# More products of a constant tile on TensorE, in the old places and in new ones

## The chip, the cores and the metric

The kernel runs on one core of a Trainium2 chip. The metric is the time of one execution on the device in microseconds. TensorE (PE) multiplies, VectorE (DVE) and ScalarE (ACT) work on what it leaves in PSUM, GpSimd (POOL) is used at the start alone, and SyncE (SP) issues the DMAs. PEld stands for TensorE's weight loads, which overlap its products.

## What is computed

Attention with a position bias, and a feed-forward layer behind it:

```python
rel = pos[:, None] - pos[None, :]                      # S = 576
x = (log1p(|rel|) / log1p(max(pos[:, None], 1)))[..., None]
bias = relu(x @ w1 + b1) @ w2                          # 1 -> 32 -> 8 heads
scores = q @ k.T / sqrt(64) + bias                     # 4 batches, 8 heads
attn = exp(scores - max) / (sum + 1e-9)
x = (attn @ v) as 2304 tokens x 512
h = x @ w_in                                           # 512 -> 2048
out = (h * sigmoid(1.702 h)) @ w_out                   # 2048 -> 512
```

Inputs and output are float32. The kernel computes most products as three float16 products of split numbers (high times high, high times low, low times high).

## The kernel before, in words

The work is cut into tasks, each for one engine, with the tasks that it depends on and the buffers that it takes and gives back. A planner (class `Plan`) runs a model of the engines over them and returns one list, `plan.seq`; the kernel then issues the instructions of that list in order, so that each engine executes its own tasks in the order of the list. The numbers that decide the order are a table of priorities (`TURNS`); the change leaves it alone.

The stages, as the trace shows them:

- The **bias**: relu of the hidden layer on ScalarE and VectorE (L636, L638), products with w2 on TensorE (`products`, L662), eviction to SBUF (L674, L676), a store to a scratch tensor in DRAM and a load back that turns it by position (L683, L732). It is spread over the first 180 us, and begins the program.
- **q and k**: loaded, split and transposed, the first ones on TensorE (L771 for q, L845 and L846 for k), the others by DMA.
- The **weights** w_in and w_out: loaded by SyncE (L1227), put together and split on VectorE (L1234, L1238, L1242, L1260, L750) and ScalarE (L1258), in the first 150 us.
- **Units** u = 0, 1, 2, ...: one block of 128 rows of one pair of heads. Each has scores on TensorE (`scores`, L983), a reduction with the bias on VectorE (L992), exp on ScalarE (L1001), normalisation, a transposition and attention times V. The first eight units transpose on TensorE (`turn_pe`, L1051 and L1054, copied out at L1060 and L1066) and multiply with V in float32 (`av_direct`, L1077); the later ones are transposed by DMA and go in pairs (`av`, L1101). The result is split at L1117, L1119 and L750.
- The **feed-forward layer**: `m1` (L1311), gating on ScalarE and VectorE (L1319, L1325, L1333, L1335, L1340) and `m2` (L1352), in blocks of 256 tokens. It begins at 103 us and goes on to the end.

PSUM has a tile `sp` of four banks, two tiles `hp`, and a tile `op` of two banks.

**Fill products.** Ahead of some tasks of TensorE the kernel issues products of a constant tile `less` (written once by GpSimd) with itself. Nobody reads their result; it goes to the right half of the second `hp` tile, of which the tasks in question use the left half. The table `WARM` (L444) gives their number by the place of the task among TensorE's tasks, counted from 0:

```python
WARM = {2: 22, 3: 18, 7: 3, ...}

def fill(n, fn):
    def both():
        for _ in range(n):
            nc.tensor.matmul(h_tiles[1][:, 256:512], lhsT=less[:, 0],
                rhs=less.rearrange("p z n -> p (z n)"), start=True, stop=True)
        fn()
    return both

pieces = [t for t in plan.seq if t["eng"] == "PE"]
for i, n in WARM.items():
    pieces[i]["fn"] = fill(n, pieces[i]["fn"])
```

They are put in after the planner has run, so the planner doesn't know of them. In the profile they have line 1413. TensorE executes its products in order: a task behind a run of fills starts after it.

Of the kernel before, what the change touches and what calls it, by code (L numbers as in the profile page):

```python
# [177 lines left out]
def kernel(  # L178
# [262 lines left out]

    MAKE_AHEAD = 1
    POOL_EXP = set()
    WARM = {2: 22, 3: 18, 7: 3, 12: 4, 15: 4, 17: 5, 18: 10, 19: 10, 31: 4, 33: 4, 51: 5, 54: 5, 86: 8, 89: 24, 90: 14, 91: 2, 95: 6}  # L444

    WIDE, NARROW = 1152, 592
    PITCH = 704
# [962 lines left out]
# [3 lines that stand above are left out]
                nc.tensor.matmul(  # L1413
                    h_tiles[1][:, 256:512], lhsT=less[:, 0], rhs=less.rearrange("p z n -> p (z n)"), start=True, stop=True
                )
            fn()
        return both

    with tc.manual_schedule():
        plan.order()  # L1420
# [3 lines that stand above are left out]
# [56 lines left out]
```

## Time and profile before

| | |
|---|---|
| timed runs | 634.31, 632.13, 633.86 us; median 633.86 |
| profiled execution | 632.81 us; its span 631.0 us |
| busy in the span | TensorE 590.9, VectorE 534.3, ScalarE 377.4 us |
| mean granted clock of TensorE | 0.995 of full speed |
| fill products | 148 |

The span runs from the first to the last instruction; all times below count from its start. A row of the timeline merges equal instructions that follow each other on an engine. [...]

### The profile page before, as it was taken

To read this page: it belongs to the slowest core of one execution; us is meant where nothing else is said; L and a number is where in the kernel's file an instruction comes from. 1 tells how busy PE (TensorE), PEld (TensorE's weight loads), DVE (VectorE), ACT (ScalarE), POOL (GpSimd) and SP (SyncE) were. 2 spreads that over 40 slices of the span, in tenths; PEclk is the share of its full clock that TensorE was granted. 3 is DMA by queue.
4 is the path that set the end of the run, shared out by engine and by line. 5 is a ranking of instruction groups with operands and counts; after the bars stand their busy time and mean duration, and the time that the engine had idled before them with its cause. 6 is when DMAs were issued, how large, how long until landed. Compare 5 with 4: busy or idle time off the path is not lost.

```text
span 631.0 us, 21930 instructions
## 1 busy us (share of the span) xinstructions
PE 590.9 (94%) x9328; PEld 422.5 (67%) x9328; DVE 534.3 (85%) x1446; ACT 377.4 (60%) x836; POOL 4.9 (1%) x22
## 2 busy tenths in 40 slices
PE   7777789997999999999999899999999999999997
PEld 4545456765666667767677676776777677777874
DVE  6989999999999989989889789899797776984442
ACT  7978988788796855554556366467364534452221
POOL 3000000000000000000000000000000000000000
PEclk9989989999999999999999999999999999999999
DMA  9999996689989999999999969979979380652000
GB/s 230 301 298 314 255 253 163 157 214 210 275 228 200 167 255 225 201 188 197 196 220 223 207 154 185 177 167 192 204 154 193 65 158 35 113 116 39 35 3 35
DMA packets 254491, 113.61 MB, mean 180 GB/s; under 512 B 234036, under 2 KB 234168, under 8 KB 254392
## 3 DMA queue, kind: packets, MB, share of 16 engines
q1 hardware_dynamic: 254104, 111.84, 83.1%
q8 instruction: 73, 1.20, 0.8%
q10 hardware_dynamic: 288, 0.35, 0.2%
q14 instruction: 26, 0.21, 0.1%
HBM read 52.26 MB, written 15.61 MB: 108 GB/s over the span
## 4 chain that ended last, share of the span: by engine, by line
PE 72%; DVE 11%; ACT 8%; DMA 6%; issue 2%; POOL 0%; SPq 0%; ACTq 0%; DVEq 0%; POOLq 0%
PE hp L1311 27%; PE op L1352 25%; PE hp L1101 8%; PE sp L983 7%; ACT wide L636 3%; DVE wide L992 2%; PE sp L662 2%; DMA wide<-in_moe_w_in_dram 2%; ACT wide L1001 2%; PE sp L1352 2%; DVE wide L750 1%; DMA narrow<-in_q_dram 1%; DVE narrow L1242 1%; DVE w L750 1%; DVE narrow L1238 1%
## 5 line engine op out<-in xcount | busy, mean ns | idle before, releaser
L1311 PE MATMUL hp<-xT,w 128*64 128x256 f16 x3456 | 204.9, 273 | 1.9 <-DVE xT L750 1.4
L1311 PEld LDWEIGHTS <-w 128*64 128x64 f16 x3456 | 186.7, 110 | 20.3 <-issue 10.9
L1352 PE MATMUL op<-w,gT 128*64 128x512 f16 x1632 | 194.7, 380 | 0.6 <-issue 0.6
L1001 ACT ACTIVATE wide<-wide,sm 128x576 f32<-128x576 f32 x144 | 110.8, 770 | 66.9 <-DVE sm L992 66.2
L1352 PEld LDWEIGHTS <-gT 128*64 128x64 f16 x1728 | 95.6, 110 | 77.6 <-issue 8.2
L992 DVE CUSTOM_DVE_ANT_0 wide<-sp,wide 128x576 f32<-128x576 f32 x144 | 105.1, 752 | 5.8 <-PE sp L983 2.9
L1319 ACT ACTIVATE th<-hp 128x256 f32<-128x256 f32 x144 | 54.3, 379 | 88.8 <-PE hp L1311 74.6
L750 DVE SCALAR_TENSOR_TENSOR wide<-wide,sm,wide 128x576 f16<-128x576 f32 x128 | 102.7, 813 | 2.6 <-ACT wide L1030 2.4
L1325 DVE SCALAR_TENSOR_TENSOR th<-th,hp 128x256 f32<-128x256 f32 x144 | 59.8, 417 | 32.3 <-ACT th L1319 30.9
L983 PE MATMUL sp<-wide,narrow 64*128 64x512 f16 (+2 forms) x720 | 65.0, 318 | 7.3 <-DVE narrow L750 2.7
L1340 DVE TENSOR_TENSOR gT<-th,gT 128x256 f16<-128x256 f32 x144 | 60.3, 421 | 10.1 <-ACT gT L1333 8.1
L1101 PEld LDWEIGHTS <-v 128*64 128x64 f16 x2160 | 57.8, 111 | 7.4 <-issue 4.7
L1101 PE MATMUL hp<-wide,v 128*64 128x128 f16 (+1 forms) x2160 | 60.2, 214 | 2.0 <-issue 2.0
L1030 ACT ACTIVATE wide<-wide,sm 128x576 f16<-128x576 f32 x72 | 54.1, 769 | 12.6 <-DVE sm L1010 10.4
L983 PEld LDWEIGHTS <-narrow 64*128 64x128 f16 (+1 forms) x960 | 28.3, 97 | 43.1 <-issue 22.6
L636 ACT ACTIVATE wide<-tab,bp 128x384 f32<-128x384 f32 (+16 forms) x94 | 56.3, 654 | 0.0
L1333 ACT CAST gT<-th 128x256 f16<-128x256 f32 x71 | 28.4, 400 | 25.9 <-DVE th L1325 14.7
L1028 DVE TENSOR_SCALAR wide<-wide,sm 128x576 f16<-128x576 f32 x56 | 28.4, 514 | 0.3
L1001 ACT ACTIVATION_READ_ACCUMULATOR wide<-wide,sm 128x1 f32 x144 | 27.2, 189 | 0.0
L662 PE MATMUL sp<-wide,pk 128*32 128x512 f32 (+24 forms) x264 | 20.9, 431 | 4.9 <-DVE sm L992 4.6
L1335 DVE CAST gT<-th 128x256 f16<-128x256 f32 x73 | 20.9, 289 | 5.1 <-PE sp L1352 3.5
L1008 DVE TENSOR_SCALAR sm<-sm 128x1 f32<-128x1 f32 (+1 forms) x128 | 18.9, 151 | 5.8 <-ACT wide L1001 5.3
(87 smaller groups left out, 489.3 us busy)
## 6 DMA issues: line engine op xcount, KB each, us to landing
wide<-scr SPq DMA_DIRECT2D x32, 576.0 KB, 5.4
scr<-narrow SPq DMA_DIRECT2D x30, 295.5 KB, 4.5
wide<-in_moe_w_out_dram SPq DMA_DIRECT2D x16, 512.0 KB, 5.6
wide<-in_moe_w_in_dram SPq DMA_DIRECT2D x16, 512.0 KB, 6.2
narrow<-in_q_dram SPq DMA_DIRECT2D x16, 256.0 KB, 4.3
out_dram<-narrow SPq DMA_DIRECT2D x15, 256.0 KB, 2.9
w<-in_v_dram SPq DMA_DIRECT2D x4, 576.0 KB, 6.9
wide<-scr SPq DMA_DIRECT2D x8, 288.0 KB, 4.6
```

The costliest lines, as they stand in the source:

```text
L636: nc.scalar.activation(out=h, in_=tv, func=ACTF.Relu, bias=bp[:, pb:pb + 1])
L750: nc.vector.scalar_tensor_tensor(out=out, in0=in0, scalar=scale, in1=in1, op0=ALU.mult, op1=ALU.subtract)
L983: nc.tensor.matmul(pair[64 * e:64 * e + m, a, cs], lhsT=qt[r, x, hp + e, q0:q0 + m], rhs=k_of(b, hp + e, y, cs)[r], start=i == 0, stop=i == 2,
L992: nc.vector.tensor_tensor_reduce(out=slot(("a32", u))[:, cs], in0=slot(("sp", u)).rearrange("p (h a) n -> p h (a n)", h=2)[:, a, 0:S], in1 ...
L1001: nc.scalar.activation(out=t, in_=t, func=ACTF.Exp, scale=-1.0, bias=sm[:, a:a + 1], accum_out=sm[:, 2 + a:3 + a])
L1030: nc.scalar.activation(out=o, in_=t, func=ACTF.Identity, scale=r)
L1101: nc.tensor.matmul(o[64 * a:64 * a + 64, po], lhsT=vt[:, x, vc:vc + 64], rhs=t[:, 9 * y + k0, po], start=kb < 0 and i == 0, stop=kb == 3 a ...
L1311: nc.tensor.matmul(p[y0:y0 + FF, :n], lhsT=wi16[:, f // 4, cc, z, w0:w0 + FF], rhs=r, start=i == 0, stop=i == 11, skip_group_check=FF < 128,)
L1319: nc.scalar.activation(out=slot(("th", j, f))[:, :n], in_=slot(("hp", j, f))[:, :n], func=ACTF.Tanh, scale=0.851 / (XS * WIS))
L1325: nc.vector.scalar_tensor_tensor(out=th, in0=th, scalar=1.0, in1=slot(("hp", j, f))[:, :n], op0=ALU.add, op1=ALU.mult)
L1340: nc.vector.tensor_tensor(out=gt[:, 1, :n], in0=th, in1=gt[:, 0, :n], op=ALU.subtract)
L1352: nc.tensor.matmul(o_of(j, i)[y0:y0 + FF], lhsT=gt[:, z, 128 * i + y0:128 * i + y0 + FF], rhs=wo16[:, NF - 1 - f, y, :], start=f == 0 and ...
```

## The change

One line: the numbers of `WARM`.

```diff
-    WARM = {2: 22, 3: 18, 7: 3, 12: 4, 15: 4, 17: 5, 18: 10, 19: 10, 31: 4, 33: 4, 51: 5, 54: 5, 86: 8, 89: 24, 90: 14, 91: 2, 95: 6}
+    WARM = {2: 24, 3: 20, 7: 4, 8: 2, 9: 2, 12: 4, 14: 1, 15: 5, 17: 7, 18: 12, 19: 12, 27: 1, 31: 5, 33: 5, 36: 3, 40: 2, 44: 2, 49: 1, 51: 6, 54: 6, 86: 9, 89: 24, 90: 16, 91: 3, 95: 7}
```

148 products become 183. Fifteen entries of the old table grow by one or two, two stay, and eight are new. What the changed entries stand ahead of, with the start of that task in the trace of before:

| entry | task behind the fills | starts at, us | fills before, now |
|---|---|---|---|
| 2, 3 | bias products of chunk 0 | 10.90, 14.14 | 22 to 24, 18 to 20 |
| 7, 8, 9 | bias products of chunk 0 | 20.47, 22.55, 25.18 | 3 to 4, 0 to 2, 0 to 2 |
| 14 | bias product of chunk 1 | 33.12 | 0 to 1 |
| 15 | scores u = 0 | 37.56 | 4 to 5 |
| 17 | bias product of chunk 1 | 41.95 | 5 to 7 |
| 18 | scores u = 1 | 44.54 | 10 to 12 |
| 19 | bias product of chunk 1 | 48.70 | 10 to 12 |
| 27 | bias product of chunk 1 | 57.63 | 0 to 1 |
| 31 | transposes of k | 63.51 | 4 to 5 |
| 33 | transposes of u = 2 | 68.73 | 4 to 5 |
| 36, 40 | attention times V, u = 2 and 3 | 71.17, 75.90 | 0 to 3, 0 to 2 |
| 44 | transposes of k | 82.17 | 0 to 2 |
| 49 | attention times V, u = 5 | 88.93 | 0 to 1 |
| 51, 54 | transposes of u = 6 and 7 | 92.76, 96.65 | 5 to 6, 5 to 6 |
| 86 | scores u = 14 | 138.77 | 8 to 9 |
| 90 | scores u = 15 | 152.30 | 14 to 16 |
| 91 | attention times V, u = 12 and 13 | 153.47 | 2 to 3 |
| 95 | `m2` of f = 9 | 160.63 | 6 to 7 |

Nothing else moves: the other engines have the same instructions in the same order. Two places, as the programs have them (rows with + are new, rows with - are gone; what an instruction waits for stands in brackets).

TensorE at entry 44, ahead of the transposes of k (`sp<-idn,w`), behind the transposes of u = 4 (`hp<-idn`, `op<-idn`):

```order
 L1051 MATMUL hp_124<-idn,wide_84 128x128 [waits Activation_49]
 L1054 MATMUL op<-idn,wide_84 128x128 x4
+L1413 LDWEIGHTS less
+L1413 MATMUL hp_124<-less 128x256
+L1413 LDWEIGHTS less
+L1413 MATMUL hp_124<-less 128x256
 L845 MATMUL sp<-idn,w_63 128x128 [waits DMAHW4_49,DVE_49,Activation_49]
```

The two fills wait for nothing; the wait stays with the first transpose.

TensorE at entry 36, ahead of attention times V of u = 2 (`hp_123<-w`), behind the scores of u = 4 (`sp<-wide,narrow`):

```order
 L983 MATMUL sp<-wide_91,narrow_107 128x64
-L1077 MATMUL hp_123<-w_63 64x128 [waits Activation_49]
-L1077 MATMUL hp_123<-w_63 64x128
+L1413 LDWEIGHTS less
+L1413 MATMUL hp_124<-less 128x256 [waits Activation_49]
+L1413 LDWEIGHTS less
+L1413 MATMUL hp_124<-less 128x256
+L1413 LDWEIGHTS less
+L1413 MATMUL hp_124<-less 128x256
+L1077 MATMUL hp_123<-w_63 64x128 x2
 L1077 MATMUL hp_123<-w_63 64x128 [waits Activation_49]
```

Here the first fill has taken over the wait of the product behind it: ScalarE copies the left half of the same tile, `hp_124`, to SBUF (L1066). The wait of the third product (for the other copy, L1060) stays. Entries 40 and 49 look alike; at entry 27 the first fill waits for VectorE's copy of that tile.

## Rows read from the trace of the kernel before

**Rows 1.** The page, busy time by engine and granted clock in 40 slices.

```profile
PE 590.9 (94%) x9328; PEld 422.5 (67%) x9328; DVE 534.3 (85%) x1446; ACT 377.4 (60%) x836; POOL 4.9 (1%) x22
...
PEclk9989989999999999999999999999999999999999
```

**Rows 2.** Windows by stage: start to end and length, busy us (instructions) by engine, clock, DMA.

```profile
0.00:100.00 100.00, 75.72 (x892) 49.95 (x894) 90.56 (x213) 85.66 (x165) 4.90 (x22) 0.97 0.98 271
...
165.00:625.00 460.00, 454.42 (x7538) 328.03 (x7536) 379.02 (x1079) 239.68 (x556) 0.00 (x0) 1.00 0.81 159
```

**Rows 3.** Timeline of TensorE: start, us, line, tiles, form, count [idle before, releaser].

```profile
25.18 1.34 PE L662 MATMUL op<-wide,pk 128*32 128x111 f32 x24 [0.54 <-ACT wide L674]
...
37.56 1.34 PE L983 MATMUL sp<-wide,narrow 64*128 64x512 f16 x12 [2.68 <-DVE narrow L750]
...
38.83 2.20 PE L662 MATMUL op<-wide,pk 128*32 128x191 f32 x24
...
41.95 1.21 PE L662 MATMUL op<-wide,pk 128*32 128x175 f32 x24
...
44.54 0.91 PE L983 MATMUL sp<-wide,narrow 64*128 64x512 f16 x12 [0.17 <-DVE sm L992]
```

**Rows 4.** Windows of half a microsecond around the two places of low clock.

```profile
38.00:38.50 0.50, 0.50 (x6) 0.24 (x4) 0.47 (x3) 0.33 (x1) 0.00 (x0) 0.50 0.08 33
...
81.50:82.00 0.50, 0.00 (x0) 0.00 (x0) 0.50 (x3) 0.50 (x3) 0.00 (x0) 1.00 0.77 303
...
82.50:83.00 0.50, 0.50 (x5) 0.50 (x4) 0.50 (x3) 0.50 (x2) 0.00 (x0) 0.50 0.98 203
```

**Rows 5.** Timeline of TensorE: runs of fill products, and the first bias product.

```profile
6.34 4.63 PE L1413 MATMUL hp<-less 128*128 128x256 f16 x22
...
10.90 1.24 PE L662 MATMUL op<-wide,pk 128*32 128x15 f32 x24
...
43.09 1.27 PE L1413 MATMUL hp<-less 128*128 128x256 f16 x10
...
142.70 2.79 PE L1413 MATMUL hp<-less 128*128 128x256 f16 x24
```

**Rows 6.** Timeline of TensorE: attention times V of u = 2, its later part.

```profile
72.08 1.09 PE L1077 MATMUL hp<-w 128*64 128x128 f32 x16 [0.47 <-ACT w L1060]
```

**Rows 7.** The chain of waits in order of time: start, us, what.

```profile
8.36 3.89 ACT wide L636 x6
...
12.26 0.71 ACT narrow L674
...
26.34 7.46 DMA wide<-in_moe_w_in_dram
...
56.66 4.18 DMA wide<-in_moe_w_in_dram
...
159.88 0.81 PE hp L1413 x6
```

**Rows 8.** Timeline of TensorE from 82 to 89 us.

```profile
82.17 1.02 PE L845 MATMUL sp<-idn,w 128*128 128x128 f32 x4 [1.06 <-ACT wide L636]
...
84.61 1.91 PE L1077 MATMUL hp<-w 64*64 64x128 f32 x20
...
87.88 0.91 PE L983 MATMUL sp<-wide,narrow 64*128 64x512 f16 x12 [0.22 <-DVE wide L750]
...
88.93 1.46 PE L1077 MATMUL hp<-w 64*64 64x128 f32 x20
```

**Rows 9.** Timeline of TensorE behind the fills at 153 and 160 us.

```profile
153.47 1.86 PE L1101 MATMUL hp<-wide,v 128*64 128x128 f16 x60
...
160.63 2.84 PE L1352 MATMUL op<-w,gT 128*64 128x512 f16 x24
```

**Rows 10.** Waits of ScalarE from 0 to 110 us: total us, times, longest.

```profile
ACT narrow L674 <- PE op L662: 2.8, 1, 2.8
```

**Rows 11.** Windows: the stage from 84 to 88 us.

```profile
84.00:88.00 4.00, 3.78 (x35) 3.00 (x35) 3.97 (x8) 2.41 (x5) 0.00 (x0) 0.79 0.95 277
```

## The prediction

> **What bounds the kernel now.** I read the page first, then busy time by stage, then the chain of waits, then TensorE's own timeline at the places that the change touches. TensorE is busy for 590.9 of 631.0 us [rows 1]. By stage [rows 2] this splits in two: from 165 to 625 us it is busy 454.4 of 460 us, and nothing of the change lies there. From 0 to 100 us it is busy only 75.7 of 100 us, while VectorE is busy 90.6. The added products stand in that first stretch (30 of 35) and in 100 to 165 us (5). So TensorE is the bound later, and in the stretch that is edited it mostly waits for VectorE, ScalarE and loads. A gain must come through that first stretch, by work that somebody else waits for.
>
> What the products can act on is the clock. In the page's row of the clock the slices from 32 to 47 and from 79 to 95 us stand below the rest [rows 1]. [...] So the prize, were both low stretches gone, is what they cost.
>
> **The price of one product.** All fill products have one form. A run of 24 takes 2.79 us and a run of 10 takes 1.27 us [rows 5], so one costs (2.79 - 1.27) / 14 = 0.109 us. In the first run of the program 22 take 4.63 us, 0.21 each [rows 5]: by its price that run is at the lower level, whatever level the page's row gives for it. The change adds 35, two of which sit in that slow first run: 33 x 0.109 + 2 x 0.21 = 4.0 us of TensorE time. That is the upper bound of the cost, if no gap takes any of it; the lower bound is nothing, because 30 of them fall into a stretch with 24.3 us of idle TensorE [rows 2].
>
> **Place by place.** I went through the timeline at all 23 entries that change. Thirty products go where the next product of the program has idle time in front of it, or within its first few, and the fill ends inside it. The tightest is in front of the scores of u = 1: the run that starts at 43.09 [rows 5] has twelve products instead of ten, and 43.09 + 12 x 0.109 = 44.40 us, against the scores' start at 44.54 [rows 3]. The place before u = 2's attention-times-V product is different: there the new products wait for the copy of the same PSUM tile, so they do not start in the gap ahead of it but after it, three of them 0.33 us long, and the cover is the next gap, 0.47 us before the x16 row [rows 6]. If that cover were gone the 0.33 us would be paid by ScalarE's and VectorE's split of that product, not by a score. The one with u = 3 is alike, with two products. These I cost at nothing.
>
> Five products are not covered. (1) The two that lengthen the first run of 22. The first bias product starts when the run is done (10.90 us, 1.24 us long [rows 5]); its eviction follows on ScalarE at 12.26 us, directly after relus that fill the time from 8.36 on, and both are on the chain [rows 7]. The product's end, 10.90 + 1.24 = 12.14, moves by 0.22 to 0.43 us, so ScalarE's eviction moves by 0.22 - 0.12 = 0.10 us up to 0.43 - 0.12 = 0.31 us. ScalarE has idle time later (below), so of this between 0 and 0.3 survive; I take 0.1. (2) One before u = 5's attention-times-V product, whose row at 88.93 us has no idle time [rows 8]: 0.11 us on TensorE, none of it on the chain, and I take 0. (3) One before u = 12's attention-times-V pair (153.47 us, no idle time ahead) and (4) one before the feed-forward layer's second product (m2) of f = 9 (160.63 us, no idle ahead) [rows 9]. The run of fills before (4) is itself a step of the chain (159.88 us [rows 7]). I take 0.11 for it, and 0 for (3), whose bounds are 0 and 0.11. Cost: 0.1 + 0.11, about +0.2 us, with ends 0 and 4.0.
>
> **What the low stretches are worth.** The first: scores u = 0 take 1.34 us where 0.91 is normal, and a bias product takes 2.20 where 1.21 is normal [rows 3]: 0.43 + 0.99 = 1.42 us, and ScalarE waits 2.8 us for that bias product [rows 10]. This one is worth up to 1.4 us. But the change puts one product ahead of an idle stretch of 2.68 us, 0.11 us of it, so I expect this fall to stay. The second: two new products go into the 1.06 us of idle time just ahead of K's transposes at 82.17 us [rows 8], and nearer to the fall there is no other place. I expect this fall to go in an execution that is timed like this one. From 82.17 to 84.61 all work is at the lower level, 2.44 us of which at most half, 1.22, comes back, and the attention-times-V product takes 1.91 instead of 1.46 [rows 8], so 1.7 us of TensorE time at most. Who waits for it? VectorE does not: it is busy 3.97 of the 4 us from 84 to 88 [rows 11], and the next scores, at 87.88 us, wait for VectorE's part of K [rows 8]. So of the 1.7 us I take 0; the ends are 0 and 1.7. What is late next is VectorE, which has no idle time to give.
>
> **The sum.** 632.8 us for the profiled execution + 0.2 - 0 = 633.0. That execution lies 1.05 us under the median of the three timed runs (633.86), and these spread over 2.2 us. The mean of all four is (634.31 + 632.13 + 633.86 + 632.81) / 4 = 633.28; on that level the forecast is 633.28 + 0.2, about **633.5 us**. About 0.3%, 1.9 us, is what a measurement of this kernel can tell from no change, so: no difference.
>
> **Rivals.** *Both falls go, and what they cost comes back.* For it: three microseconds of half speed twice, the first of them on the chain. Against: 0.11 us in a gap of 2.68, and VectorE's full windows. Time: 633.28 - 1.42 - 1.7 = 630.2 us; with only the first gone, 631.9.
>
> *The falls lie elsewhere in the timed runs.* In the trace the clock's places are those of one execution, and the spread of 2.2 us between runs is as large as one low stretch can be worth, so another run may have falls that this trace lacks; the products in other gaps would then work there. Time: one low stretch fewer in each run, paid in full, 633.28 - 1.7 = 631.6 us. [...]
>
> *A load that the chain waits for comes late (slower).* The load of a w_in tile is on the chain twice, once 7.46 us long from 26.34 us and once 4.18 us [rows 7]. The chain steps to the first from the bias product that starts at 25.18 us after 0.54 us of idle time [rows 3], and the change puts two products in front of it. If these delay the release so far that the load falls in behind another transfer, the difference of the two rows, 3.3 us, is the price: 633.28 + 3.3 = 636.6 us. Against: that idle time is more than twice the fill. It decides from the point where the delay of the release exceeds 0.54 - 0.22 = 0.32 us. Without a load, more than 1.9 / 0.109 = 17 of 35 products would have to be uncovered, and I count 5.
>
> *The change doesn't do what it says.* The fills that wait for a copy fill no gap; that holds at four entries with seven products, costs at most 0.3 us more and lies within the forecast.
>
> **How the numbers follow.** No difference: 0.68. Faster by over 0.3%: 0.18, from the first two rivals (0.07 and 0.11). Slower by over 0.3%: 0.14, from the late load (0.10) and from fills that are uncovered in places where I saw cover (0.04). The range: below, to 631.6, where one fall is paid back in full; above, to 635.2, about 1.9 us over the mean, which takes in the greater part of the 4.0 us bound without the late load. That leaves out some 1 in 10 on either side.
>
> **What would show it.** Right: TensorE's fills are 183 products in place of 148; the clock still reads 0.50 once near 38 us and not at 82 us; VectorE is as full as before from 80 to 88 us; the stretch from 165 us on is as long as before. Wrong for the gain: no window under 1.00 after 12 us, and the first product of the 460 us stretch over 1.9 us earlier. Wrong for the cost: ScalarE or VectorE with new waits for bias products or transposes behind a fill, or a load on the chain that is longer than 7.46 us. The forecast falls if the median differs by over 1.9 us either way.

## The result and the profile after

The changed kernel takes 638.58 us (median of 11 runs, 634.89 to 640.10), the kernel before in the same comparison 633.27 us (11 runs): a ratio of 1.0076, 95% interval 1.0052 to 1.0101. It is slower by 0.5 to 1.0%. The forecast was 633.5 us, "no difference", with a range from 631.6 to 635.2: the result lies above the range, and the difference is clear of the noise. A second comparison (below) gave 1.0042, interval 1.0019 to 1.0066. The profiled execution of the changed kernel took 638.7 us, its span 636.9.

The page of the changed kernel: busy time, the clock in 40 slices, the instruction queue, and the group of the fill products.

```profile
PE 597.7 (94%) x9363; PEld 428.5 (67%) x9363; DVE 534.8 (84%) x1446; ACT 377.0 (59%) x836; POOL 4.9 (1%) x22
...
PEclk9999899998999999999899999999999999999999
...
q8 instruction: 73, 1.20, 0.8%
...
L1413 PE MATMUL hp<-less 128*128 128x256 f16 x183 | 27.4, 298 | 1.8 <-ACT w L1066 1.1
```

The fills are 183, and TensorE has 35 products and 35 weight loads more than in [rows 1]: 70 instructions. Its busy time grew by 6.8 us, though 35 fills are worth 4.0 by the prediction's price. The rows of single products overlap: 183 of 298 ns would be 54.5 us, and the group is busy for 27.4.

Windows of the changed kernel: the first stage of [rows 2], the two places of [rows 4], and four places of low clock (start to end and length, busy us by engine, clock, DMA share, GB/s).

```profile
0.00:100.00 100.00, 76.91 (x916) 50.80 (x918) 90.43 (x213) 85.55 (x164) 4.87 (x22) 0.98 0.98 271
...
38.00:38.50 0.50, 0.50 (x12) 0.25 (x8) 0.50 (x2) 0.50 (x2) 0.00 (x0) 1.00 0.71 287
82.50:83.00 0.50, 0.50 (x6) 0.50 (x7) 0.50 (x3) 0.50 (x3) 0.00 (x0) 1.00 0.75 173
64.00:64.50 0.50, 0.50 (x4) 0.50 (x5) 0.50 (x4) 0.50 (x2) 0.00 (x0) 0.77 1.22 358
149.50:150.00 0.50, 0.50 (x6) 0.16 (x3) 0.47 (x4) 0.50 (x2) 0.00 (x0) 0.60 1.18 218
310.00:311.00 1.00, 1.00 (x23) 0.56 (x9) 1.00 (x3) 0.41 (x1) 0.00 (x0) 0.51 1.35 218
334.00:335.00 1.00, 1.00 (x8) 0.78 (x5) 0.69 (x4) 1.00 (x4) 0.00 (x0) 0.50 1.22 274
```

Both low stretches of [rows 4] are gone in this execution: the two windows read 1.00 in place of 0.50, which is the lower level that the prediction speaks of. Others have come, at 64 (0.77) and 149.5 us (0.60), and at 310 (0.51) and 334 us (0.50), far behind the last place that the diff touches.

Timeline of TensorE in the changed kernel: the first fills, the bias product of entry 17 [rows 3], `m2` of f = 9 [rows 9], and 309 to 367 us.

```profile
6.33 4.40 PE L1413 MATMUL hp<-less 128*128 128x256 f16 x24
10.65 1.24 PE L662 MATMUL op<-wide,pk 128*32 128x15 f32 x24
...
40.73 1.21 PE L662 MATMUL op<-wide,pk 128*32 128x175 f32 x24
...
161.44 2.78 PE L1352 MATMUL op<-w,gT 128*64 128x512 f16 x24
...
309.36 0.41 PE L983 MATMUL sp<-wide,narrow 64*64 64x512 f16 x4 [2.01 <-DMA narrow<-narrow]
...
326.83 2.09 PE L1101 MATMUL hp<-wide,v 128*64 128x64 f16 x120
328.75 1.48 PE L1311 MATMUL hp<-xT,w 128*64 128x256 f16 x23
332.66 0.27 PE L1311 MATMUL hp<-xT,w 128*64 128x256 f16 x1 [2.42 <-issue]
332.66 4.29 PE L1352 MATMUL op<-w,gT 128*64 128x512 f16 x24
336.59 3.23 PE L1311 MATMUL hp<-xT,w 128*64 128x256 f16 x48
...
355.54 0.38 PE L1101 MATMUL hp<-wide,v 128*64 128x64 f16 x13 [0.34 <-issue]
...
367.01 1.47 PE L1352 MATMUL op<-w,gT 128*64 128x512 f16 x12
```

The same work in the timeline of the kernel before (rows that did not stand above).

```profile
321.31 2.09 PE L1101 MATMUL hp<-wide,v 128*64 128x64 f16 x120
323.23 1.48 PE L1311 MATMUL hp<-xT,w 128*64 128x256 f16 x24
324.54 2.76 PE L1352 MATMUL op<-w,gT 128*64 128x512 f16 x24
328.22 2.81 PE L1311 MATMUL hp<-xT,w 128*64 128x256 f16 x48 [0.93 <-DVE xT L750]
...
349.52 0.59 PE L1352 MATMUL op<-w,gT 128*64 128x512 f16 x3 [0.59 <-issue]
...
354.34 0.67 PE L1101 MATMUL hp<-wide,v 128*64 128x64 f16 x31 [0.24 <-issue]
...
360.54 0.92 PE L1101 MATMUL hp<-wide,v 128*64 128x64 f16 x47 [1.77 <-issue]
361.29 1.47 PE L1352 MATMUL op<-w,gT 128*64 128x512 f16 x12
```

Set side by side, these rows tell where the time went. Starts of the same work, changed minus before (in brackets the same for a second execution of the changed kernel, of the run f1_again below):

| work | before, us | later by, us |
|---|---|---|
| `m2` of f = 9 | 160.63 | 0.81 (0.07) |
| scores at | 305.45 | 3.91 (1.72) |
| 120 products of attention times V | 321.31 | 5.52 (2.71) |
| `m1`, 48 products | 328.22 | 8.37 (6.91) |
| `m2`, 12 products | 361.29 | 5.72 (3.54) |
| end of the span | 631.0 | 5.9 (3.7) |

At the last edited place (`m2` of f = 9) the changed kernel is only 0.81 and 0.07 us behind. The largest step within a few microseconds is, in both executions, the one from 321 to 328 us of the kernel before, where nothing was edited and each engine has the same work in the same order. The new thing there is a wait of 2.42 us of TensorE for its own instructions ("issue"), in the middle of a run of `m1`, followed by products at a granted clock of 0.50 (window 334 to 335 us; 24 of `m2` in 4.29 us instead of 2.76). The chain of waits of the changed kernel runs through it:

```profile
328.92 1.31 PE hp L1311 x23
330.23 2.42 issue
332.66 0.27 PE hp L1311
```

### The profile page after: what moved, and what is told of

Read it like the earlier page. It is cut to its first block, busy times and chain, and to the rows that moved or that the text cites. A ratio compares the mean times of both kernels' runs of the same rounds, so it can differ in the third digit from the quotient of the medians.

```text
span 636.9 us, 21998 instructions
## 1 busy us (share of the span) xinstructions
PE 597.7 (94%) x9363; PEld 428.5 (67%) x9363; DVE 534.8 (84%) x1446; ACT 377.0 (59%) x836; POOL 4.9 (1%) x22
## 4 chain that ended last, share of the span: by engine, by line
PE 71%; DVE 13%; DMA 7%; ACT 5%; SPq 2%; issue 2%; DVEq 0%; ACTq 0%
PE hp L1311 26%; PE op L1352 25%; PE hp L1101 7%; PE sp L983 7%; DVE wide L992 3%; PE sp L662 2%; PE sp L1352 2%; DVE wide L750 2%; ACT wide L1001 1%; ACT wide L636 1%; DMA wide<-in_k_dram 1%; DVE narrow L1238 1%; DVE w L750 1%; DVE narrow L1242 1%; DMA w<-in_v_dram 1%
## 5 line engine op out<-in xcount | busy, mean ns | idle before, releaser
L1311 PE MATMUL hp<-xT,w 128*64 128x256 f16 x3456 | 207.2, 275 | 3.6 <-issue 2.4
L1352 PEld LDWEIGHTS <-gT 128*64 128x64 f16 x1728 | 97.6, 110 | 78.3 <-issue 9.6
L1413 PE MATMUL hp<-less 128*128 128x256 f16 x183 | 27.4, 298 | 1.8 <-ACT w L1066 1.1
```

What stands on the lines that cost most here:

```text
L1311: nc.tensor.matmul(p[y0:y0 + FF, :n], lhsT=wi16[:, f // 4, cc, z, w0:w0 + FF], rhs=r, start=i == 0, stop=i == 11, skip_group_check=FF < 128,)
L1352: nc.tensor.matmul(o_of(j, i)[y0:y0 + FF], lhsT=gt[:, z, 128 * i + y0:128 * i + y0 + FF], rhs=wo16[:, NF - 1 - f, y, :], start=f == 0 and ...
```

## The experiments

**Where TensorE waits for instructions.** I numbered TensorE's instructions in order of their start: products, weight loads and its few semaphore instructions (some 40) alike. The page's instruction queue q8 moved 73 packets and 1.20 MB, so 16 KB each, in either kernel; 2 x 9363 instructions make 73.1 pieces of 256. In the kernel before, the waits at 349.52, 354.34 and 360.54 us are at instructions 9665, 9921 and 10177; in the changed kernel those at 332.66 and 355.54 are at 8897 and 9665. All are whole multiples of 256 apart, and that held for all 29 such waits of TensorE's products over 0.2 us in the 14 profiled executions of this study. So I call these places the cuts of the stream. (The changed kernel and those made from it have two semaphore instructions fewer, so their cuts lie two instructions beside the shifts named below: 68 in place of 70.)

**The theory** (COUNT in the expectations): TensorE's instructions come in pieces of 256, and it waits where it has run through a piece before the next is there. 70 added instructions move all later cuts by 70 against the work. Before, the cut near 322 us falls into the 120 products of attention times V (240 instructions with their weight loads, 2.09 us in all; the burst, from here on): 99 of these stand in one piece, 141 in the next. After, 209 of them and the 47 that follow make up one piece, which runs through in 3.15 us. **The rivals:** the added products themselves, at their places (PLACES: time on TensorE, or other work that comes later because of them); and the clock.

Windows of the changed kernel, from cut to cut: first the piece with the burst, then a short piece with no wait at its end.

```profile
327.08:332.66 5.58, 3.15 (x142) 2.89 (x135) 3.98 (x12) 1.77 (x4) 0.00 (x0) 1.00 1.22 144
...
361.47:365.71 4.24, 4.24 (x141) 3.01 (x134) 4.24 (x12) 1.25 (x3) 0.00 (x0) 1.00 0.46 127
```

The first is 3.15 us of work and a wait to 5.58; the second, 4.24 us long, has none. So a short piece alone does not make the wait. What does is in the DMA records of the traces: when the 16 KB packet of each piece started and how long it took. The first packet belongs to the cut at 449, the second to the cut at 705, and so on. A window of 0.05 us in the DMA view shows one packet; here are those of the piece behind the burst, in the changed kernel (329.50 to 329.55 us) and before (324.60 to 324.65):

```profile
q8 instruction: 1, 0.02, 241.0%
```

```profile
q8 instruction: 1, 0.02, 164.9%
```

The share is that of 16 engines in the window, so the first took 2.41 x 16 x 0.05 = 1.93 us and the second 1.32. Set against the cuts:

| piece | cut before it, us | its packet starts, takes, us | TensorE goes on, us | after the packet's end, us | wait, us |
|---|---|---|---|---|---|
| before, behind the burst | 322.09 | 324.64, 1.32 | 328.66 | 2.70 | none |
| before, at 360.54 us | 354.34 | 358.08, 0.98 | 360.54 | 1.48 | 1.77 |
| changed, behind the burst | 327.08 | 329.52, 1.93 | 332.66 | 1.21 | 2.42 |
| f1_again, behind the burst | 324.24 | 326.74, 2.60 | 330.82 | 1.48 | 3.43 |
| changed, the short piece | 361.47 | 362.00, 1.44 | 365.71 | 2.27 | none |

At all 29 waits TensorE went on 1.21 to 1.61 us after the end of its packet, and at none of 1010 cuts in the 14 traces did it go on sooner than 1.21 us after it. So the wait is for the packet. It starts near the time at which TensorE passes the cut before (between 3.1 us ahead of it and 5.7 us behind), so it comes about one piece ahead, and at these waits the piece had run through before its packet was there: at the changed kernel's burst, 3.15 us of work, and the packet's end 4.37 us behind the cut. The kernel before had a packet as late at the burst (started 2.55 us behind the cut, against 2.44), but there the piece in front of it ran for 6.57 us. How late a packet is goes with the DMA traffic: with a DMA share under 0.5 around the cut it ended 0.73 us behind the cut (median of 223 pieces), with 0.9 and more 2.35 us (603 pieces). That the traffic is the cause is argued; no run changed it alone.

**e1_halves: 70 instructions more, no time more.** The kernel before, with 35 of its fills cut into two halves:

```diff
+    HALVES = {89: 24, 90: 11}
...
+                    for z in range(2):
+                        nc.tensor.matmul(h_tiles[1][:, 256 + 128 * z:384 + 128 * z],
+                            lhsT=less[:, 0], rhs=less[:, z], start=True, stop=True)
```

> The numbers of before, but the 24 products of entry 89 and 11 of the 14 of entry 90 are cut into two products of half the columns each: 35 products and 70 instructions more from 143 us on, as in the changed kernel, with nothing added before 143 us and no extra columns. Theory COUNT (70 more instructions on TensorE move the places at which it waits for its own instructions into a worse stretch; the places of the fills do not matter): about as slow as the changed kernel, 636.5 to 640 us, with an idle time of over 2 us ended by issue near 333 us. Theory PLACES (the added products hold up the tasks behind them): as before, within 2 us of it, since the halves lie in idle stretches of 2.5 and 1.2 us.

636.73 us against 634.46, ratio 1.0036 (1.0014 to 1.0059): slower, without one of the change's products. Its timeline has the wait at the same cut, and at entry 89 48 halves take what 24 whole fills took [rows 5]:

```profile
143.44 2.85 PE L1416 MATMUL hp<-less 128*128 128x128 f16 x48
...
331.94 0.42 PE L1311 MATMUL hp<-xT,w 128*64 128x256 f16 x2 [2.85 <-issue]
```

**e2_early and e3_late: the change in two parts.** e2 has only the new numbers up to entry 54 (30 products, 60 instructions), e3 only those from entry 86 on (5 products, 10 instructions):

```diff
# e2_early, against the changed kernel
-    ... 86: 9, 89: 24, 90: 16, 91: 3, 95: 7}
+    ... 86: 8, 89: 24, 90: 14, 91: 2, 95: 6}
# e3_late, against the kernel before
-    ... 86: 8, 89: 24, 90: 14, 91: 2, 95: 6}
+    ... 86: 9, 89: 24, 90: 16, 91: 3, 95: 7}
```

> The 30 added products of the first 100 us alone (entries 2 to 54), 60 instructions more. PLACES: if the loss comes from the first stretch, 636 to 640 us, and the first product behind 165 us is later than before by the loss; if it comes from entries 86 to 95, as before, within 2 us. COUNT: near the changed kernel, 636 to 640 us, but with a loss behind 250 us and none at 150 us.

> The five added products of entries 86, 90, 91 and 95 alone, 10 instructions more. PLACES: if these hold up the work at 140 to 161 us, +0.5 us there and what follows from it, up to 638 us; else as before. COUNT: 10 instructions move little, within 2 us of before.

e2: 636.83 us, 1.0047 (1.0025 to 1.0069); e3: 633.75 us, 0.999 (0.9967 to 1.0013). The early part carries the loss. In e2's timeline the wait is at the same cut; e3 has none there, only the later ones of the kernel before:

```profile
333.07 2.35 PE L1352 MATMUL op<-w,gT 128*64 128x512 f16 x20 [2.37 <-issue]
```

```profile
350.79 1.05 PE L1352 MATMUL op<-w,gT 128*64 128x512 f16 x8 [1.43 <-issue]
...
361.26 1.01 PE L1101 MATMUL hp<-wide,v 128*64 128x64 f16 x52 [1.25 <-issue]
```

**e4_realign: the change, and 93 small products more.** They bring the shift from 70 to 256 instructions, so that the cuts lie again where they lay:

```diff
+    SMALL = {15: 30, 19: 23, 89: 40}
...
+            for _ in range(small):
+                nc.tensor.matmul(h_tiles[1][0:64, 256:320], lhsT=less[:, 0, 0:64],
+                    rhs=less[:, 0, 0:64], start=True, stop=True)
```

> The changed kernel with 93 small products (64 rows of weights, 64 columns) more, in idle stretches at entries 15, 19 and 89, so that TensorE has 256 instructions more than before in all. COUNT, with fetches in pieces of 256 instructions (four idle times ended by issue in the two traces stand at the same place modulo 256): the later stage has the places of before again, so within 2 us of before, 631 to 636 us. PLACES: as slow as the changed kernel or slower, 637 to 642 us.

634.08 us, 0.9999 (0.9975 to 1.0024). With all 35 products of the change and 93 more the loss is gone. Its timeline has the small run, no wait between the burst and what follows, and the old waits behind:

```profile
143.78 1.45 PE L1418 MATMUL hp<-less 128*64 128x64 f16 x40
...
319.82 2.09 PE L1101 MATMUL hp<-wide,v 128*64 128x64 f16 x120
321.74 1.48 PE L1311 MATMUL hp<-xT,w 128*64 128x256 f16 x24
323.05 2.76 PE L1352 MATMUL op<-w,gT 128*64 128x512 f16 x24
...
347.22 0.41 PE L1352 MATMUL op<-w,gT 128*64 128x512 f16 x2 [0.59 <-issue]
```

**f1_again, f4_minus35: the change once more, and without its shift.** f4 keeps the early new products and takes 35 others out at 143 to 150 us (entry 89 gone, entry 90 from 16 to 5), so that the count is the old one from 161 us on.

```diff
-    ... 86: 9, 89: 24, 90: 16, 91: 3, 95: 7}
+    ... 86: 9, 90: 5, 91: 3, 95: 7}
```

> The changed kernel once more, beside the others of this series. Its first comparison gave a ratio of 1.0076 with an interval of 1.0052 to 1.0101. COUNT: 3 to 4 us over before (1.004 to 1.007), with an idle time of 2 to 3 us ended by issue near 333 us, as in the two shifted kernels of the series before (they lay 2.3 and 3.0 us over it). PLACES would have it 5 us over, as the first comparison did.

> The changed kernel with 35 products fewer at entries 89 (none) and 90 (5 of 16), so that the instruction count is that of before from 153 us on. All other added products stay. COUNT: as before, within 2 us, perhaps up to 1.7 us slower for a clock that falls near 148 us. PLACES: as slow as the changed kernel, 4 to 5 us over before, since 30 of the 35 added products are there.

f1: 637.35 us against 634.24, 1.0042 (1.0019 to 1.0066). f4: 634.69 us, 1.0014 (0.9986 to 1.0042). f4's interval reaches up to the repeat's ratio, so its time alone would settle nothing; its trace has no wait for instructions before 356.87 us. The repeat's timeline:

```profile
324.02 2.09 PE L1101 MATMUL hp<-wide,v 128*64 128x64 f16 x120 [0.92 <-DVE th L1325]
325.92 1.48 PE L1311 MATMUL hp<-xT,w 128*64 128x256 f16 x23
330.82 0.27 PE L1311 MATMUL hp<-xT,w 128*64 128x256 f16 x1 [3.43 <-issue]
330.83 4.54 PE L1352 MATMUL op<-w,gT 128*64 128x512 f16 x24
```

**f2_plus55, f3_plus128: the kernel before with small products alone.** The first adds 110 instructions, the second 256 and more work.

```diff
+    SMALL = {15: 20, 19: 15, 89: 20}   # f2_plus55
+    SMALL = {15: 45, 19: 33, 89: 50}   # f3_plus128
```

> The numbers of before and 55 small products (64 rows of weights, 64 columns, 0.033 us each) in idle stretches at entries 15, 19 and 89: 110 instructions more, 1.8 us of TensorE time that lies in 6 us of idle time. COUNT: of all shifts between 0 and 254 this is among the worst: laid over the trace of before, the pieces of 256 instructions then hold bursts at 323, 360, 524 and 580 us that run in less than the 5.4 us that a fetch took, in sum about 5 us more than before: 636 to 641 us. PLACES: as before, within 2 us.

> The same with 128 small products in the same three places: 256 instructions more, 4.2 us of TensorE time in the same idle stretches. COUNT: the cuts lie where they lay before, so as before within 2 us, and faster than the kernel with 55 although it has more to do. PLACES, or any cost of the products themselves: slower than the kernel with 55.

f2: 636.31 us, 1.003 (1.0006 to 1.0054), at the lower end of what I expected: of the bursts at 323, 360, 524 and 580 us that I had counted on, only the first made a wait. f3: 634.45 us, 0.9995 (0.9976 to 1.0015). The larger addition costs nothing and the smaller one does: the shift decides, not the number of products. f2's cut lies two products into `m1`; f3 has two of the three waits of before, the last one to the hundredth:

```profile
327.26 0.28 PE L1311 MATMUL hp<-xT,w 128*64 128x256 f16 x2
330.60 2.56 PE L1311 MATMUL hp<-xT,w 128*64 128x256 f16 x22 [3.06 <-issue]
```

```profile
349.87 0.59 PE L1352 MATMUL op<-w,gT 128*64 128x512 f16 x3 [0.69 <-issue]
...
360.62 0.92 PE L1101 MATMUL hp<-wide,v 128*64 128x64 f16 x47 [1.77 <-issue]
```

**g1 to g4: other shifts, one execution each.** The kernel before with 10, 20, 35 and 80 small products:

```diff
+    SMALL = {15: 4, 19: 3, 89: 3}      # g1_plus10
+    SMALL = {15: 8, 19: 6, 89: 6}      # g2_plus20
+    SMALL = {15: 13, 19: 9, 89: 13}    # g3_plus35
+    SMALL = {15: 28, 19: 22, 89: 30}   # g4_plus80
```

> Before with 10 small products (20 instructions) in idle stretches. One look, for the idle times ended by issue. COUNT, worked out from the trace of before as 5.4 us less the time in which a piece of 256 instructions runs: 0 to 0.6 us near 327 us, 2.7 us near 348 us, 1 us near 358 us; 633 to 636 us. If the stall near 330 us has another cause than the cut, it is there in full or not at all, whatever the shift.

> The same with 20 small products (40 instructions). COUNT: 1.4 us near 326 us, 3.0 us near 347 us; 634 to 637 us.

> The same with 35 small products (70 instructions): the instruction count of the changed kernel without any of its products. COUNT: 2.6 us near 325 us (2.4 to 3.4 were seen with a shift of 60 to 110), 2.4 us near 347 us; 635 to 639 us. PLACES: no stall near 325 to 333 us, since none of the added products is there.

> The same with 80 small products (160 instructions). COUNT: the cuts now end pieces at 323, 356 and 359 us: 2.5, 1.7 and 2.4 us; 635 to 640 us.

635.79, 639.28, 636.77 and 637.42 us, one execution each, beside one of the kernel before at 631.82. One execution is no verdict on a time, and g1 is 4 us above that one though it has no wait near 330 us; what I take from these runs is the place of the waits. Their sizes I had mostly wrong: g1 had 0.83 us at 350.89 in place of 2.7, g3 none in place of 2.4 near 347, g4 0.40 in place of 2.5 near 323, and g2's time lies above its range. The expectations took 5.4 us for every fetch (e4 shows 5.37, from the cut at 347.22 to 352.59 us); from the cut before to where TensorE went on, the 29 waits show 3.4 to 6.6 us. The rows of g2 (first), g3 and g4, one fence each:

```profile
333.55 1.46 PE L1352 MATMUL op<-w,gT 128*64 128x512 f16 x11 [1.34 <-issue]
```

```profile
330.87 0.42 PE L1311 MATMUL hp<-xT,w 128*64 128x256 f16 x2 [2.33 <-issue]
```

```profile
325.92 0.54 PE L1101 MATMUL hp<-wide,v 128*64 128x64 f16 x23 [0.40 <-issue]
...
364.11 2.19 PE L1352 MATMUL op<-w,gT 128*64 128x512 f16 x11 [3.14 <-issue]
```

All fourteen traces, by their shift against the kernel before:

| shift at 320 us, instructions | wait at the cut behind the burst, us | timed ratio |
|---|---|---|
| 0: before; f4 | none; none | 1; 1.0014 |
| 10, 20: e3; g1 | none; none | 0.999; - |
| 40, 60: g2; e2 | 1.34; 2.37 | -; 1.0047 |
| 70: changed; f1; e1; g3 | 2.42; 3.43; 2.85; 2.33 | 1.0076; 1.0042; 1.0036; - |
| 110: f2 | 3.06 | 1.003 |
| 160: g4 | 0.40, and 3.14 at 364 us | - |
| 256: e4; f3 | none; none | 0.9999; 0.9995 |

The wait for instructions is there in seven of seven traces with a shift of 40 to 110, and in none of six at 0 to 20 or 256. The five timed comparisons with it have intervals above 1; the four without it have intervals that hold 1. None of the versions is faster than the kernel before.

## Why the prediction was wrong

**The step that failed** is "from 165 to 625 us it is busy 454.4 of 460 us, and nothing of the change lies there", with its test "the stretch from 165 us on is as long as before". No product of the change lies there, but the change moves the cuts of TensorE's stream through all of it. The late stretch grew by 5.9 - 0.8 = 5.1 us in the profiled execution and by 3.7 - 0.1 = 3.6 in the repeat. That term, the time in which TensorE waits for its own instructions, was zero in the sum and none of the rivals had it; the runs put 2.42 and 3.43 us of such waiting where before there was none, and products at a clock of 0.50 behind it; nor did I ask why TensorE, in its tightest stretch, waits 1.77 us for nothing at 360.54 us, a wait which was there to be read in the trace of before.

**What of it is shown.** e1 (shift, no time added), f2 and f3 (fewer products cost, more do not) and e4 (all products of the change, no loss) tell the shift from the products. The clock has a part at most: it falls to 0.50 behind the wait in the changed kernel, e1, f1 and f2, but not in e2 (1.00 from 333.5 to 334.5 us), which loses as much. That the wait is a fetch of instructions that comes late is shown by the packets of the instruction queue, 16 KB to 256 instructions: TensorE went on 1.21 to 1.61 us after the end of its packet at all 29 waits, and at none of 1010 cuts sooner than 1.21. At the other 981 cuts it had no such wait; at the 29 it stood still for 0.2 to 3.4 us.

**How the loss adds up.** From the burst to the `m1` behind it the repeat loses 6.91 - 2.71 = 4.20 us: 3.43 of wait and 4.54 - 2.76 = 1.78 behind it, at a clock of 0.50 (332 to 334 us), less 0.93 us that the kernel before waits there for VectorE, 4.28. In the profiled execution it is 2.85 by the rows, 2.42 + 1.53 - 0.93 = 3.02 by the same sum. Later some comes back, since the waits at 349 to 361 us (0.59 + 0.24 + 1.77 = 2.60) become 0.34, or none in the repeat. So the waits for instructions are not much longer in sum (2.60 us before, 2.76 and 3.43 after), but lie elsewhere; in the new place they cost more, and a part of that is the clock, which falls behind them: to 0.50 there in the changed kernel, e1, f1, f2 and g3, while behind the waits of before it stays at 1.00. In e2 and g2 it doesn't fall (1.00 in g2 from 334 to 335 us), but there the later waits stay too, 4.8 and 4.0 us in sum.

**Not settled:** the part before the burst, 5.52 - 0.81 = 4.7 us in the profiled execution and 2.6 in the repeat. Rows show a wait for q's transposition by DMA (2.01 us at 309.36, with the window 310 to 311 at 0.51 behind it; 1.24 us in the repeat) that at this place neither the kernel before nor e3, e4, f3 and f4 have. It comes with the shift in all shifted traces but e2's, and in g1's, and no run took it alone. A late arrival at the burst is not lost in itself: f4 starts the 120 products at 325.40 us, 4.09 us late, and its span is only 0.6 us longer than before, for behind the burst it has neither the wait for VectorE nor more than one wait for instructions.

**Step by step.** *The price at the places:* +0.2 us forecast; the last place, `m2` of f = 9, comes 0.81 us later in one execution and 0.07 in the other, around the forecast, and the first bias product 0.25 us earlier in one (10.65 us) and 0.13 later in the other (11.03). e3, with the five late products, is at 0.999. Right within what can be told. That the first run of fills is at the lower level was my estimate from its price alone: the windows of before from 6.30 to 10.90 us read 1.00. *The two falls of the clock:* I expected the first to stay and the second to go. In the repeat that is so (0.50 from 38 to 41 us, 1.00 from 82 to 83). In the profiled execution both went (1.00 in both windows), and a bias product came 1.21 us earlier for it (40.73 us against 41.95 [rows 3]), but the scores of u = 1 only 0.05 (44.49 against 44.54). That the products act on the clock was argued, and is not shown. *What the falls are worth:* little, as forecast, but not shown to be nothing. e4's profiled execution has no fall (mean clock 1.000) and is 631.0 - 629.3 = 1.7 us shorter; e4's twelve timed runs give 0.9999, but their mean clocks lie between 0.990 and 1.000, so most have falls too. In the 69 timed runs of the kernel before that stood beside the e and f runs, those with a mean clock of 0.999 and more took 632.9 us (8 runs) and those under 0.990 took 635.8 us (10 runs); this goes together, and what causes what is not shown. *Falls that lie elsewhere in other executions:* right as a fact (in two executions of the changed kernel at 64, 150, 310 and 334 us, and at 38, 147 and 331 us), but it brought no gain. *The late load:* the step on the chain that was 7.46 us [rows 7] is 6.75 us in the changed kernel, so this rival, the only slower one, didn't happen. VectorE's covers and the fills that take over a wait are as the prediction had them: ScalarE's longest wait for a bias product fell from 2.8 [rows 10] to 0.7 us.

## What to carry to other kernels

Here 70 instructions added to TensorE moved every later 256-instruction cut of its stream, also where the code is untouched, and put a wait of 2.42 and 3.43 us where there was none before. So number an engine's instructions and see which waits for "issue" stand on a common step. With a burst of 240 short instructions in 2.09 us and shifts of 40 to 110, TensorE waited for 1.3 to 3.4 us behind the burst (in the changed kernel at a DMA share of 1.22), and in five of the seven traces the clock fell to 0.50 behind the wait: look for both. Whether a wait is a late fetch can be read from the packets of the instruction queue; here TensorE went on 1.21 to 1.61 us after the end of its packet. A comparison of two kernels that differ in count should have a control that restores the count with harmless instructions, as e4 does, before the edit itself is blamed.

## What the runs showed of the hardware

- TensorE's products waited for instructions 29 times over 0.2 us in 14 executions, for 0.2 to 3.4 us, at places that lie whole multiples of 256 instructions apart.
- TensorE went on 1.21 to 1.61 us after the end of the 16 KB packet that belongs to the piece, and at none of 1010 cuts sooner. A packet took 0.9 to 2.6 us and started about one piece ahead.
- The wait is not a fixed price: a piece of 4.24 us with the DMA share at 0.46 had none, a piece with 3.15 us of work at 1.22 had 2.42, and f4, with the cuts of before, had only one wait of 0.94 us where before has three.
- 40 small products (64 columns, weights 128 by 64) took 1.45 us, 0.036 us each, so 93 of them moved a stream by 186 instructions for about 3.4 us of TensorE in gaps, at no measurable cost.
